# Attention and spatial gating on one core: a new plan of all calls, and the first batch's attention output copied out of PSUM before it is split

## The chip, the cores and the metric

The kernel runs on one core of one Trainium2 chip. The metric is device time of one execution in microseconds. The times shown are the median of three runs and their ends.

## The reference

The input is q, k, v of 4 batches x 8 heads x 768 positions x 64, all in float32. The attention is banded with a few global columns, and the output feeds a gated MLP with a spatial product over the positions:

```python
scores = q @ k.T / 8 - slope[h] * dist          # keep: column < n_global, or 0 <= row - col < n_local
a = softmax(where(keep, scores, -1e9))           # n_global = 8, n_local = 96
x = (a @ v), heads side by side                  # (4, 768, 512)
h = relu(x @ w_in)                               # w_in 512 x 1024; u, v = halves of h
v_n = (v - mean(v)) / sqrt(var(v) + 1e-6)        # over the 512 features
v_s = w_spatial @ v_n + b_spatial                # over the 768 positions
out = (u * v_s) @ w_out                          # w_out 512 x 512
```

w_in and w_out come as float64 and are read as pairs of 32-bit words.

## The kernel before

A batch is cut into six blocks of 128 positions, so there are 24 blocks n. With a band of 96 a block of queries needs its own block of keys and the one before, 256 columns in all; the global columns are copied into the previous block's first columns (kg into kring). Per block the steps are: P fetches q and k, W fetches v, S computes scores (PSUM tile s), evicts them on DVE with the bias and a running extreme (pr, mn), takes the exponential on ACT with a row sum, normalises (pr by rc), and A transposes the weights on TensorE (PSUM tile p), copies them to SBUF (pth), and multiplies with v (PSUM tile ops). Batch 0 does this with float32 operands. Batches 1 to 3 split k, q, v, and the transposed weights into a high and a low half in a reduced-precision format, by a cast and a subtraction (hi_lo), and gather q and k by DMAs through raw and rawh. Every x is split into xth and xtl.

The MLP runs over those halves with three products each (high x high, high x low, low x high): V gives v and its normalisation (row statistics st, mv, rs, then vnh, vnl), U gives u, G the spatial product over w_t (spatial weights) with the bias b_bc and the product with u, split into gh and gl, and O the output product with w_out. V is per block, U, G and O per 256 positions. Their PSUM tile is m, and ev is a ring of three staging tiles in SBUF. The weights are prepared during batch 0: I and Q split w_in and w_out (a bit-level conversion from float64, about ten 512- or 256-wide operations a piece, mostly on DVE), T splits w_spatial, B fetches the bias. The tiles u, raw, rawh and m serve the weights too, and blocks 4 and 5 of batch 0 keep their x in the tiles gh and gl.

No engine is programmed in the order of the source. A recorder keeps every call (that is why each row of the profile says line 39, where calls are issued), and a planner, run when the kernel is built, simulates five engines and a DMA queue with a cost for each call and puts the calls of each engine in the order in which its simulation starts them. Three tables steer it. KEYS gives each step a rank, and at equal readiness the lower one goes first. CFG says by letter which engine takes a kind of call: a (ACT), v (DVE), p (GpSimd, called POOL), or x, where the planner chooses; a string of several letters is taken in turn. The costs are in cost, reach and plan. Afterwards keep_warm looks at TensorE's planned gaps over a size, and fills them with transposes of the identity into a PSUM tile that nobody uses at that time (fillers: their only input is ident).

Of the kernel before, what the change touches and what calls it, by code (L numbers as in the profile page):

```python
# [263 lines left out]
def reach(op, o, eng, end, stand):  # L264

    if op.eng == "sync":
        return end if eng == "sync" and op.num not in o.after else stand + 50 + SLACK
    if op.eng == eng:
        return stand + 95 if op.num in o.after and eng != "tensor" else end
    return stand + CROSS[op.eng][eng] + SLACK  # L270


def plan(ops, keys, trace=None):
# [28 lines left out]
    while done < n:  # L302
# [79 lines left out]
def keep_warm(order, born, make):  # L382
# [7 lines left out]
    for op in order:  # L390
        if op.eng == "tensor":
            gap = op.begun - last
            if gap > WARM_GAP and op.begun < WARM_TO:
# [13 lines left out]
                if best and best[0] < last:  # L407
                    out.extend(make(best[1]) for _ in range(int((gap - 300) // 112)))
# [6 lines left out]
WORDS = {"gh": 1024, "gl": 1024, "pth": 1024, "vring": 3072, "kring": 2048, "pr": 256, "s": 512, "p": 512, "m": 512, "ops": 1024, "q0": 1024, "q1": 1024}  # L415
BUFS = {"gh": 1, "gl": 1, "u": 3, "s": 2, "p": 2, "m": 2, "raw0": 1, "raw1": 1, "rawh0": 1, "rawh1": 1}
SLACK = 120
KEYS = {('P', 0): 1.1, ('bias', 0): -1.7, ('S', 0): 0.03, ('bias', 1): 0.4, ('P', 1): 1.3, ('A', 0): -1.26, ('S', 1): 0.53, (0, 'T', 0): 1.88, (0, 'T', 1): 2.42, ('P', 2): 1.8, ('A', 1): 1.3, ('S', 2): 0.53, (0, 'V', 0): 1.99, (0, 'T', 2): 2.88, (0, 'T', 3): 2.38, ('P', 3): 2.3, ('A', 2): 2.3, ('S', 3): 3.03, ('W', 3): 3.2, (0, 'V', 1): 3.99, (0, 'U', 0): 2.14, (0, 'T', 4): 5.75, (0, 'T', 5): 3.88, ('P', 4): 4.99, ('A', 3): 3.3, ('S', 4): 3.53, ('W', 4): 2.77, (0, 'V', 2): 3.99, (0, 'Q', 0): 3.0, (0, 'Q', 1): 3.0, ('P', 5): 3.3, ('A', 4): 4.3, ('S', 5): 4.53, (0, 'V', 3): 4.99, (0, 'U', 1): 6.14, (0, 'Q', 2): 4.0, (0, 'Q', 3): 6.5, ('P', 6): 5.12, ('A', 5): 5.3, ('S', 6): 3.5, ('W', 6): 6.08, (0, 'V', 4): 5.99, (0, 'V', 5): 5.9, (0, 'U', 2): 8.14, ('P', 7): 5.62, ('A', 6): 6.04, ('S', 7): 6.0, ('W', 7): 7.08, (0, 'G', 0): 6.7, (0, 'O', 0): 6.5, ('P', 8): 7.12, ('A', 7): 6.96, ('S', 8): 5.5, ('W', 8): 8.58, (0, 'G', 1): 7.7, ('P', 9): 8.12, ('A', 8): 7.96, ('S', 9): 5.5, ('W', 9): 9.58, (0, 'G', 2): 8.7, (1, 'V', 0): 9.0, (1, 'V', 1): 9.34, (1, 'U', 0): 11.38, ('P', 10): 8.62, ('A', 9): 8.96, ('S', 10): 8.5, ('W', 10): 10.58, (1, 'V', 2): 10.0, ('P', 11): 10.12, ('A', 10): 9.96, ('S', 11): 9.5, ('W', 11): 11.08, (1, 'V', 3): 11.0, (1, 'U', 1): 12.0, ('P', 12): 10.13, ('A', 11): 10.96, ('W', 12): 13.08, (1, 'V', 4): 11.0, (1, 'V', 5): 13.0, (1, 'U', 2): 13.0, ('P', 13): 13.12, ('A', 12): 12.96, ('S', 13): 11.59, ('W', 13): 13.08, (1, 'O', 0): 14.16, ('P', 14): 13.12, ('A', 13): 12.96, ('S', 14): 12.5, ('W', 14): 13.08, (1, 'O', 1): 15.16, ('P', 15): 13.32, ('A', 14): 12.55, ('S', 15): 13.5, ('W', 15): 14.58, (1, 'G', 2): 15.0, (1, 'O', 2): 16.16, (2, 'U', 0): 16.5, ('P', 16): 15.12, ('A', 15): 14.96, ('S', 16): 15.71, ('W', 16): 15.55, ('P', 17): 15.62, ('A', 16): 15.96, ('S', 17): 15.5, ('W', 17): 15.58, (2, 'V', 3): 16.66, ('P', 18): 16.62, ('S', 18): 16.0, ('W', 18): 17.58, (2, 'V', 4): 17.0, (2, 'V', 5): 19.0, (2, 'U', 2): 19.5, ('P', 19): 18.12, ('A', 18): 17.96, ('S', 19): 17.5, ('W', 19): 17.29, (2, 'O', 0): 22.66, ('P', 20): 19.12, ('A', 19): 17.96, ('S', 20): 18.5, ('W', 20): 19.58, (2, 'G', 1): 19.5, (2, 'O', 1): 18.81, ('P', 21): 25.11, ('A', 20): 20.46, ('S', 21): 19.0, ('W', 21): 22.51, (2, 'G', 2): 21.0, (2, 'O', 2): 21.16, (3, 'V', 0): 18.71, (3, 'V', 1): 19.5, (3, 'U', 0): 23.74, ('P', 22): 20.62, ('A', 21): 20.96, ('S', 22): 20.5, ('W', 22): 22.08, (3, 'V', 2): 22.0, ('P', 23): 22.62, ('A', 22): 22.46, ('S', 23): 21.56, ('W', 23): 25.7, (3, 'V', 3): 22.5, (3, 'U', 1): 24.0, ('A', 23): 22.46, (3, 'V', 4): 23.0, (3, 'V', 5): 24.0, (3, 'O', 0): 25.16, (3, 'G', 1): 22.5, (3, 'O', 1): 25.85, (3, 'G', 2): 23.5, (3, 'O', 2): 27.12}
WARM_FROM, WARM_GAP, WARM_TO = 3000.0, 900.0, 150000.0
# [3 lines left out]
def attn_then_spatial_gating_kernel(  # L423
# [185 lines left out]
    def split_weights(src, hi, lo, st, x):  # L609
# [228 lines left out]
    def values(n):  # L838
# [23 lines left out]
        for g in range(NP):  # L862
# [7 lines left out]
            if whole(n):  # L870
# [322 lines left out]
```

## Time and profile before

| | |
|---|---|
| median of three runs | 508.26 us (506.62 to 509.0) |
| profiled execution | 506.37 us, span 504.6 us |
| TensorE (PE) busy | 481.6 us, 95% |
| VectorE (DVE) busy | 371.9 us, 74% |
| ScalarE (ACT) busy | 283.2 us, 56% |
| GpSimd (POOL) busy | 266.6 us, 53% |
| granted TensorE clock | 0.996 of full |

Times in the profile are in microseconds from the span's start; a mean time of one instruction is in nanoseconds. A row of a group gives line, engine, operation, output<-inputs, shapes and count, then busy time and mean, then the idle time of the engine just ahead and what ended it. In the windows the numbers behind a stretch are busy times of PE, the weight loads, DVE, ACT and POOL, with their instruction counts, then the granted clock, the DMA share and GB/s. Busy time of PE includes fillers.

### The profile page before, as it was taken

The numbers are of one execution on the slowest core, as the hardware profiler recorded it, in microseconds if no ns is written. First come the engines' busy times: TensorE is split into PE (matmuls) and PEld (weight loads), VectorE is DVE, ScalarE is ACT, GpSimd is POOL, SyncE is SP. The second block draws the span as 40 slices with busy tenths as digits, with TensorE's granted clock in tenths as the row PEclk, the third lists the DMA queues.
The fourth block names the chain that finished last, engine by engine and source line by source line (L and its number), as shares of the span: only waits on it lengthen the run. The fifth ranks groups of instructions, "written<-read, shape, count | busy, mean of one in ns | idle before, by whom it ended". The sixth has DMA issues, their size and how long they took to land.

```text
span 504.6 us, 10144 instructions
## 1 busy us (share of the span) xinstructions
PE 481.6 (95%) x3297; PEld 436.6 (87%) x3297; DVE 371.9 (74%) x1082; ACT 283.2 (56%) x779; POOL 266.6 (53%) x403
## 2 busy tenths in 40 slices
PE   8888999999998999999999999999989999999995
PEld 8776778879887988899989899998979989999994
DVE  5999979888478897787988765779877657743232
ACT  4568766653355777776667635777766516531111
POOL 3167544246446676789775634889765516241000
PEclk9899999999999999999999999999999999999999
DMA  6985510223776677666766626765657610000111
GB/s 203 286 202 144 142 33 20 70 60 107 177 191 160 161 200 202 163 174 163 179 162 178 184 73 170 199 170 148 168 128 206 163 58 1 12 2 1 43 43 48
DMA packets 68846, 65.51 MB, mean 130 GB/s; under 512 B 6736, under 2 KB 50000, under 8 KB 68784
## 3 DMA queue, kind: packets, MB, share of 16 engines
q1 hardware_dynamic: 68784, 64.78, 49.0%
q8 instruction: 28, 0.46, 0.4%
q14 instruction: 34, 0.28, 0.2%
HBM read 29.76 MB, written 6.68 MB: 72 GB/s over the span
## 4 chain that ended last, share of the span: by engine, by line
PE 68%; DVE 12%; DMA 6%; POOL 5%; ACT 4%; issue 2%; SPq 1%; POOLq 0%; ACTq 0%; DVEq 0%
PE m L39 49%; PE ops L39 8%; PE s L39 6%; PE p L39 5%; DVE ev L39 2%; DVE pr L39 2%; DMA raw<-in_k_dram 2%; POOL pr L39 2%; DMA kring<-raw 2%; ACT pr L39 2%; SPq L39 1%; DVE m L39 1%; DVE rawh L39 1%; DVE raw L39 1%; POOL raw L39 1%
## 5 line engine op out<-in xcount | busy, mean ns | idle before, releaser
L39 ACT ACTIVATE pr<-pr,mn 128x256 f32<-128x256 f32 (+1 forms) x192 | 92.0, 481 | 28.7 <-DVE mn L39 28.3
L39 POOL TENSOR_SCALAR pr<-pr,rc 128x256 f32<-128x256 f32 (+1 forms) x173 | 83.5, 503 | 8.1 <-DVE rc L39 6.5
L39 PE MATMUL s<-kring,q 128*128 128x256 f32 (+1 forms) x384 | 69.9, 307 | 6.1 <-DVE mn L39 4.3
L39 DVE CUSTOM_DVE_ANT_0 pr<-s,bias 128x256 f32<-128x256 f32 (+1 forms) x192 | 68.6, 395 | 7.6 <-PE s L39 6.3
L39 DVE TENSOR_TENSOR c<-ops,c 64x256 f32<-64x256 f32 x144 | 60.5, 420 | 14.2 <-ACT c L39 10.7
L39 PE MATMUL ops<-pth,vring 128*128 128x256 f32 x352 | 64.9, 313 | 4.8 <-ACT pth L39 1.4
L39 ACT ACTIVATE pth<-p 128x512 fp32r<-128x512 f32 (+3 forms) x96 | 52.4, 559 | 28.7 <-PE p L39 21.7
L39 PEld LDWEIGHTS s<-kring,q 128*128 128x128 f32 x384 | 56.0, 192 | 11.2 <-DVE mn L39 5.4
L39 PEld LDWEIGHTS ops<-pth,vring 128*128 128x128 f32 x352 | 50.6, 189 | 13.5 <-ACT pth L39 4.7
L39 PE MATMUL p<-ident,pr 128*128 128x128 f32 x352 | 58.2, 274 | 1.5 <-DVE pr L39 1.1
L39 DVE TENSOR_TENSOR pth<-p,pth 128x512 fp32r<-128x512 f32 (+1 forms) x72 | 45.8, 641 | 14.3 <-ACT pth L39 13.7
L39 PEld LDWEIGHTS p<-ident,pr 128*128 128x128 f32 x352 | 42.3, 140 | 8.0 <-DVE pr L39 1.6
L39 PE MATMUL m<-w_t_h,vnl 128*128 128x256 f32 x288 | 44.6, 282 | 0.0
L39 POOL TENSOR_TENSOR xtl<-c,xth 128x256 fp32r<-128x256 f32 x36 | 27.9, 775 | 31.5 <-ACT xth L39 31.3
L39 PE MATMUL m<-w_t_h,vnh 128*128 128x256 f32 x288 | 44.2, 284 | 0.0
L39 PE MATMUL m<-w_t_l,vnh 128*128 128x256 f32 x288 | 43.7, 282 | 0.0
L39 ACT ACTIVATE ev<-m 128x512 f32<-128x512 f32 (+1 forms) x37 | 21.5, 583 | 38.3 <-PE m L39 31.1
L39 POOL TENSOR_TENSOR vnl<-ev,vnh 128x512 fp32r<-128x512 f32 x24 | 31.5, 1313 | 19.0 <-ACT vnh L39 11.4
L39 PEld LDWEIGHTS m<-w_t_h,vnh 128*128 128x128 f32 x288 | 38.4, 189 | 0.7 <-ACT u L39 0.2
L39 DVE TENSOR_TENSOR ev<-m,b_bc 128x512 f32<-128x512 f32 x24 | 16.5, 689 | 30.4 <-PE m L39 30.3
L39 PEld LDWEIGHTS m<-w_t_h,vnl 128*128 128x128 f32 x288 | 38.5, 189 | 0.0
L39 PEld LDWEIGHTS m<-w_t_l,vnh 128*128 128x128 f32 x288 | 38.0, 189 | 0.0
(126 smaller groups left out, 1030.1 us busy)
## 6 DMA issues: line engine op xcount, KB each, us to landing
q<-rawh SPq DMA_DIRECT2D x72, 128.0 KB, 2.4
q<-raw SPq DMA_DIRECT2D x72, 128.0 KB, 2.4
out_dram<-ev SPq DMA_DIRECT2D x23, 256.0 KB, 2.7
raw<-in_q_dram SPq DMA_DIRECT2D x36, 128.0 KB, 3.0
raw<-in_v_dram SPq DMA_DIRECT2D x18, 256.0 KB, 3.3
raw<-in_k_dram SPq DMA_DIRECT2D x36, 128.0 KB, 3.0
kring<-rawh SPq DMA_DIRECT2D x36, 128.0 KB, 2.5
kring<-raw SPq DMA_DIRECT2D x36, 128.0 KB, 2.6
```

Of the source, the lines that this page charges most:

```text
L39: getattr(self.real, self.call)(*self.args, **self.kw)
```

## The change

All tables are replaced. CFG gets entries that hold for one batch only (a name with @ and the number), so that an engine choice can differ between batches; KEYS are new in nearly all entries. The planner's model of the DMA queue becomes a function, with an issue that can be held up by a full queue; keep_warm fills gaps from 500 ns of plan on instead of 900, and more densely. In the first batch the attention output is copied from PSUM to an SBUF tile (xs, of the ring c) and split there, in two whole 128 x 256 operations per pair of head pairs, where before each half of the partitions was split out of PSUM. The masking and the low word's scaling in the weight flush get a variant for GpSimd.

```diff
-CFG = {'vrelu': 'a', ... 'x0h': 'a', 'x0l': 'v', ... 'bias0': 'xx', 'bias1': 'vx', ... 'gm': 'x', ...}
+CFG = {'wf': 'v', 'wm': 'v', 'x0': 'a', ... 'bias0@0': 'a', 'bias1@0': 'p', 'bias2@0': 'a', ... 'x0@0': 'xxvv', 'xf0h@0': 'xx', 'xf0l@0': 'x', 'wf@0': 'vvvv', ... 'gm@1': 'v', 'gm@2': 'x', 'gm@3': 'p', ...}
...
+    more = SLACK_PE if eng == "tensor" else SLACK
...
+def transfer(op, t, queue):
+
+    end = t + min(max(op.busy, queue - 4500 - t), 1300)
+    queue = max(queue, t + 1200) + (op.late - 2050)
+    return end, queue + (1400 if t > 1500 else 3400), queue
...
         if e == "sync":
-            dma = max(dma, t + 1200) + (op.late - 2050)
-            stand = dma + 1400
+            end, stand, dma = transfer(op, t, dma)
...
-                    out.extend(make(best[1]) for _ in range(int((gap - 300) // 112)))
+                    out.extend(make(best[1]) for _ in range(int((gap - 200) // 112)))
...
-WARM_FROM, WARM_GAP, WARM_TO = 3000.0, 900.0, 150000.0
+WARM_FROM, WARM_GAP, WARM_TO = 3000.0, 500.0, 150000.0
...
     def E(key, k=0):
-        x = CFG[key]
+        x = CFG.get(f"{key}@{now_in[0]}", CFG[key])
         return EN[x[k % len(x)]]
...
-        nc.vector.scalar_tensor_tensor(out=a, in0=m, scalar=UPPER_MIN, in1=a, op0=ALU.is_ge, op1=ALU.mult)
+        if E("wf", x) is nc.gpsimd:
+            nc.gpsimd.tensor_scalar(out=m, in0=m, scalar1=UPPER_MIN, scalar2=1.0, op0=ALU.is_ge, op1=ALU.mult)
+            nc.gpsimd.tensor_tensor(out=a, in0=a, in1=m, op=ALU.mult)
+        else:
+            nc.vector.scalar_tensor_tensor(out=a, in0=m, scalar=UPPER_MIN, in1=a, op0=ALU.is_ge, op1=ALU.mult)
...
                 if g % 2:
-                    if folded(n):
-                        xs = work.tile([P, 2, P], F32, name="xs", tag="c1", bufs=nb("c1"))
+                    xs = work.tile([P, 2, P], F32, name="xs", tag="c1", bufs=nb("c1"))
                     for half, s_ in enumerate(halves):
...
-                            hi_lo(src, xh[s_, gs, toks], xl[s_, gs, toks], E("x0h", half), E("x0l", half))
-                    if folded(n):
-                        hi_lo(xs, xh[:, gs, toks], xl[:, gs, toks], E("xf0h", g // 2), E("xf0l", g // 2))
+                            cp(E("x0", half), xs[s_], src)
+                    hi_lo(xs, xh[:, gs, toks], xl[:, gs, toks], E("xf0h", g // 2), E("xf0l", g // 2))
...
```

TensorE counts the same useful instructions before and after; its fillers go from 181 to 229. What the new tables make of the order shows at three places. The first is the DMA queue of SyncE at the start of the program: before, the first instructions are these (nraw are the flags n_global and n_local, u a piece of w_in, vring a block of v).

```order
L39 DMA nraw<-in_n_global_dram 128x2
L39 DMA nraw<-in_n_local_dram 128x2
L39 DMA vring_112<-in_v_dram 128x512 x2
L39 DMA u_113<-in_moe_w_in_dram 128x1024
L39 DMA u_116<-in_moe_w_in_dram 128x1024
L39 DMA u_119<-in_moe_w_in_dram 128x1024
L39 DMA q_0_94<-in_q_dram 64x4x128
L39 DMA kring_96<-in_k_dram 64x4x128
L39 DMA q_0_94<-in_q_dram 64x4x128
L39 DMA kring_96<-in_k_dram 64x4x128
```

After, they stand so:

```order
L39 DMA vring_112<-in_v_dram 128x512
L39 DMA nraw<-in_n_global_dram 128x2
L39 DMA nraw<-in_n_local_dram 128x2
L39 DMA q_0_94<-in_q_dram 64x4x128
L39 DMA kring_96<-in_k_dram 64x4x128
L39 DMA q_0_94<-in_q_dram 64x4x128
L39 DMA kring_96<-in_k_dram 64x4x128
L39 DMA u_113<-in_moe_w_in_dram 128x1024
L39 DMA u_116<-in_moe_w_in_dram 128x1024
L39 DMA u_119<-in_moe_w_in_dram 128x1024
```

The first q and k transfers moved ahead of the three pieces of w_in, and one piece of v ahead of the flags.

The second place is ACT at the first attention output of batch 0 (ops is the output in PSUM, xth its high half, c the SBUF tile of the copies, w_in_h the high half of a weight piece). Before:

```order
L39 ACTIVATE pth_124<-p_123 128x256
L39 ACTIVATE pth_126<-p_125 128x256
L39 ACTIVATE pr_129,sums_92<-pr_129,mn_127 128x256
L39 ACTIVATE xth_121<-ops_93 64x2x128
L39 ACTIVATE pr_130,sums_92<-pr_130,mn_127 128x256
L39 ACTIVATE pth_124<-p_123 128x256
L39 ACTIVATE xth_121<-ops_93 64x2x128
L39 ACTIVATE pth_126<-p_125 128x256
L39 ACTIVATE w_in_h<-m_120 128x512
```

After:

```order
L39 ACTIVATE w_in_h<-m_114 128x512
L39 ACTIVATE w_in_h<-rawh_0_118 128x512
L39 ACTIVATE pth_124<-p_123 128x256
L39 ACTIVATE pth_126<-p_125 128x256
L39 ACTIVATE xth_121<-c_0_127 128x2x128
L39 ACTIVATE c_1_132<-ops_93 64x256 x2
L39 ACTIVATE xth_121<-c_1_132 128x2x128
L39 ACTIVATE w_t_h<-vring_112 128x768
L39 ACTIVATE pr_130,sums_92<-pr_130,mn_128 128x256
```

Casts out of ops have become copies of ops to c, and the cast reads c. On DVE, at the same place, before (xtl is the low half, rawh and m hold weight pieces):

```order
L39 TENSOR_TENSOR xtl_122<-ops_93,xth_121 64x2x128
L39 SCALAR_TENSOR_TENSOR m_120<-ev_99,m_120 128x512
L39 ISA pr_103,mn_127<-s_105,bias 128x256
L39 ISA mn_127 128x1
L39 TENSOR_SCALAR raw_0_115<-m_120 128x512
L39 TENSOR_TENSOR xtl_122<-ops_93,xth_121 64x2x128
L39 TENSOR_TENSOR m_120<-m_120,w_in_h 128x512
L39 TENSOR_TENSOR w_in_l<-rawh_0_118,ev_98 128x512
```

After:

```order
L39 COPY c_0_127<-ops_93 64x256 x2
L39 TENSOR_TENSOR m_114<-m_114,w_in_h 128x512
L39 TENSOR_SCALAR rawh_0_117<-rawh_0_118 128x512
L39 TENSOR_TENSOR xtl_122<-c_0_127,xth_121 128x2x128
L39 TENSOR_TENSOR w_in_l<-m_114,ev_97 128x512
L39 TENSOR_SCALAR raw_0_115<-m_120 128x512
L39 ISA pr_130,mn_128<-s_102,bias 128x256
L39 ISA mn_128 128x1
L39 TENSOR_TENSOR xtl_122<-c_1_132,xth_121 128x2x128
```

The subtraction that read ops now reads c, for all 128 partitions at once, and is done twice where it was done four times.

The third place is the end of the program on DVE, the last two gate products (u tiles hold u here) and the output copies. Before:

```order
L39 TENSOR_TENSOR ev_97<-m_114,b_bc 128x512
L39 TENSOR_TENSOR ev_97<-ev_97,u_116 128x512
L39 TENSOR_TENSOR gl_146<-ev_97,gh_145 128x512
L39 TENSOR_TENSOR ev_98<-m_120,b_bc 128x512
L39 TENSOR_TENSOR ev_98<-ev_98,u_116 128x512
L39 TENSOR_TENSOR gl_146<-ev_98,gh_145 128x512
L39 COPY ev_99<-m_114 128x512
```

After:

```order
L39 TENSOR_TENSOR ev_97<-m_114,b_bc 128x512
L39 TENSOR_TENSOR gl_149<-ev_97,gh_148 128x512
L39 TENSOR_TENSOR ev_98<-m_120,b_bc 128x512
L39 TENSOR_TENSOR gl_149<-ev_98,gh_148 128x512
L39 COPY ev_99<-m_114 128x512
```

and on POOL, whose last instructions before were those of the normalised v (vnl), there stand now:

```order
L39 TENSOR_TENSOR vnl_162<-ev_99,vnh_161 128x512
L39 TENSOR_TENSOR ev_98<-ev_98,u_119 128x512
L39 TENSOR_TENSOR ev_99<-ev_99,u_119 128x512
L39 TENSOR_TENSOR ev_99<-ev_99,u_113 128x512
L39 TENSOR_TENSOR ev_97<-ev_97,u_113 128x512
L39 TENSOR_TENSOR ev_97<-ev_97,u_116 128x512
L39 TENSOR_TENSOR ev_98<-ev_98,u_116 128x512
```

The products of the last batch with u have left DVE's order and close POOL's.

More of the change, by code (lines that the diff above doesn't have):

```diff
@@ L264, in reach @@
 def reach(op, o, eng, end, stand):
+    more = SLACK_PE if eng == "tensor" else SLACK
     if op.eng == "sync":
-        return end if eng == "sync" and op.num not in o.after else stand + 50 + SLACK
+        return end if eng == "sync" and op.num not in o.after else stand + 50 + more
     if op.eng == eng:
         return stand + 95 if op.num in o.after and eng != "tensor" else end
-    return stand + CROSS[op.eng][eng] + SLACK
+    return stand + CROSS[op.eng][eng] + more
+def transfer(op, t, queue):
+    end = t + min(max(op.busy, queue - 4500 - t), 1300)
+    queue = max(queue, t + 1200) + (op.late - 2050)
+    return end, queue + (1400 if t > 1500 else 3400), queue
 def plan(ops, keys, trace=None):
@@ L361, in plan @@
         begun[x] = t
-        free[e] = end = t + op.busy
-        stand = end + op.late
         if e == "sync":
-            dma = max(dma, t + 1200) + (op.late - 2050)
-            stand = dma + 1400
+            end, stand, dma = transfer(op, t, dma)
+        else:
+            end = t + op.busy
+            stand = end + op.late
+        free[e] = end
         done += 1
@@ L412, in keep_warm @@
     return out
[L415 removed]
+WORDS = {"gh": 1024, "gl": 1024, "pth": 1024, "vring": 3072, "kring": 2048, "pr": 256, "s": 512, "p": 512, "m": 512, "ops": 1024, "q0": 1024, "q1": 1024, "c1": 256}
 BUFS = {"gh": 1, "gl": 1, "u": 3, "s": 2, "p": 2, "m": 2, "raw0": 1, "raw1": 1, "rawh0": 1, "rawh1": 1}
 SLACK = 120
[L418 removed]
@@ L646, in split_weights @@
         nc.vector.scalar_tensor_tensor(out=ai, in0=ci, scalar=-0x40000000, in1=ai, op0=ALU.bitwise_and, op1=ALU.bitwise_or)
-        nc.vector.scalar_tensor_tensor(out=a, in0=m, scalar=UPPER_MIN, in1=a, op0=ALU.is_ge, op1=ALU.mult)
-        nc.vector.tensor_scalar(out=ci, in0=ai, scalar1=-0x800000, scalar2=None, op0=ALU.bitwise_and)
-        nc.vector.scalar_tensor_tensor(out=m, in0=lower.bitcast(U32), scalar=2.0 ** -52, in1=c, op0=ALU.mult, op1=ALU.mult)
+        if E("wf", x) is nc.gpsimd:
+            nc.gpsimd.tensor_scalar(out=m, in0=m, scalar1=UPPER_MIN, scalar2=1.0, op0=ALU.is_ge, op1=ALU.mult)
+            nc.gpsimd.tensor_tensor(out=a, in0=a, in1=m, op=ALU.mult)
+        else:
+            nc.vector.scalar_tensor_tensor(out=a, in0=m, scalar=UPPER_MIN, in1=a, op0=ALU.is_ge, op1=ALU.mult)
+        nc.vector.tensor_scalar(out=ci, in0=ai, scalar1=-0x800000, scalar2=None, op0=ALU.bitwise_and)
+        if E("wm", x) is nc.vector:
+            nc.vector.scalar_tensor_tensor(out=m, in0=lower.bitcast(U32), scalar=2.0 ** -52, in1=c, op0=ALU.mult, op1=ALU.mult)
+        else:
+            if E("wm", x) is nc.gpsimd:
+                nc.gpsimd.tensor_scalar(out=m, in0=lower.bitcast(U32), scalar1=2.0 ** -52, scalar2=1.0, op0=ALU.mult, op1=ALU.mult)
+            else:
+                nc.scalar.activation(m, lower.bitcast(U32), AF.Copy, scale=2.0 ** -52)
+            two(None, m, m, c, ALU.mult)
         cp(E("whi"), hi, a)
@@ L1032, in attn_then_spatial_gating_kernel @@
         more = n + 1 < B * NB
+        now_in[0] = b
         for tok in CFG["S" if b == 0 else "T"][i]:
```

5 lines of the change are left out of this document (4 added, 1 removed).

## The prediction

> **What bounds the kernel now.** I read the totals and the slices of the page first, then the busy times by stage, then who waits for whom, then the groups by form.
>
> ```profile
> PE 481.6 (95%) x3297; PEld 436.6 (87%) x3297; DVE 371.9 (74%) x1082; ACT 283.2 (56%) x779; POOL 266.6 (53%) x403
> PE   8888999999998999999999999999989999999995
> DVE  5999979888478897787988765779877657743232
> ```
>
> TensorE (PE) is busy 95% of 504.6 us and DVE 74%. A mean hides two regimes, so the stages:
>
> ```profile
> 0.00:10.00 10.00, 7.60 (x56) 7.60 (x57) 4.05 (x27) 2.47 (x7) 3.74 (x14) 1.00 0.52 189
> 10.00:60.00 50.00, 43.11 (x252) 35.47 (x251) 48.87 (x155) 35.09 (x107) 27.58 (x35) 0.97 0.82 209
> 60.00:120.00 60.00, 57.51 (x338) 48.45 (x338) 52.32 (x155) 36.50 (x94) 25.22 (x36) 1.00 0.17 50
> 140.00:400.00 260.00, 255.14 (x1832) 235.91 (x1833) 207.19 (x612) 171.76 (x485) 176.31 (x270) 1.00 0.66 168
> 400.00:440.00 40.00, 40.00 (x275) 36.94 (x274) 24.44 (x64) 19.57 (x48) 15.73 (x26) 1.00 0.14 43
> 440.00:490.00 50.00, 50.00 (x358) 47.07 (x357) 19.41 (x35) 8.89 (x17) 7.50 (x11) 1.00 0.06 22
> ```
>
> The columns behind the length are PE, weight loads, DVE, ACT, POOL. From 10 to 60 us DVE is busy 48.87 of 50: it evicts the scores, splits the weights and subtracts for the low halves, and PE waits for it. From 60 to 120 both are near full (57.51 and 52.32 of 60). From 140 on PE is the bound, and from 400 it has no hole. PE's busy time in the front is partly not work: fillers, which multiply the identity into a free bank.
>
> ```profile
> L39 PE MATMUL s<-ident 128*128 128x128 f32 x133 | 16.7, 288 | 2.4 <-POOL ident masks.py:199 2.4
> L39 PE MATMUL m<-ident 128*128 128x128 f32 x48 | 6.3, 288 | 0.0
> 2.40 13.14 PE L39 MATMUL s<-ident 128*128 128x128 f32 x105 [2.40 <-POOL ident masks.py:199]
> 6.01 0.17 DVE L39 CAST nf<-nraw 128x4 f32<-128x4 int32 x1 [5.06 <-DMA nraw<-in_n_local_dram]
> 119.59 0.76 PE L39 MATMUL m<-w_t_h,vnh 128*128 128x256 f32 x5
> 118.87 0.68 DVE L39 BATCH_NORM_STATS2 st<-ev 128x6 f32<-128x512 f32 x1
> ```
>
> The 181 fillers take 23.0 us, 0.127 us each, and PE starts on a real score at 15.4 us (2.40 and 13.14). So what there is to win lies mostly before 120 us. The last two rows give the mark at which I measure the front: the sixth row statistic of the first batch ends at 119.55 us, and the first spatial matmul follows at 119.59.
>
> **The change, part by part.** The new branches that let GpSimd flush the weights are not taken: the table says DVE for both switches, and the order shows both steps on DVE. They cost nothing. What acts is the copy in the first batch, the engine choices and the order. The sum is made against the profiled execution, 506.37 us (its span is 504.6), which is 1.9 us under the median of the runs, 508.26.
>
> *DVE work ahead of that mark.* I counted DVE's instructions up to the sixth statistic in both orders, and price what differs by these rows:
>
> ```profile
> L39 DVE TENSOR_TENSOR xtl<-ops,xth 64x256 fp32r<-64x256 f32 x16 | 6.7, 419 | 4.3 <-ACT xth L39 3.3 <-PE ops L39 0.9
> L39 DVE TENSOR_TENSOR gl<-ops,gh 64x256 fp32r<-64x256 f32 x8 | 3.4, 420 | 2.3 <-PE ops L39 2.2
> L39 DVE TENSOR_SCALAR bias<-ev 128x128 bf16<-128x128 f32 x4 | 0.8, 271 | 0.0
> L39 DVE TENSOR_SCALAR bias<-ev 128x256 bf16<-128x256 f32 x4 | 1.0, 284 | 0.0
> L39 DVE TENSOR_TENSOR w_out_l<-rawh,ev 128x256 fp32r<-128x256 f32 x4 | 2.8, 688 | 0.0
> L39 DVE TENSOR_TENSOR w_out_l<-m,ev 128x256 fp32r<-128x256 f32 x4 | 1.7, 414 | 0.0
> L39 DVE TENSOR_SCALAR u<-m 128x512 f32<-128x512 f32 x5 | 3.4, 685 | 0.3 <-PE m L39 0.2
> L39 DVE TENSOR_SCALAR pr<-pr,rc 128x128 f32<-128x128 f32 x4 | 1.9, 531 | 0.0
> L39 DVE TENSOR_SCALAR pr<-pr,rc 128x256 f32<-128x256 f32 x15 | 5.5, 395 | 0.0
> ```
>
> Gone are the 24 subtractions from PSUM (6.7 + 3.4 = 10.1 us) and all eight bias scalings (1.8 us), which go to ACT and POOL: -11.9. Added are eight of the new 128x256 subtractions (POOL takes the other four). No row has this one; between the two rows of w_out_l, 0.41 us with an operand in PSUM and 0.69 with both in SBUF, I take 0.69, since both of its operands lie in SBUF: +5.5 (3.3 at the low end). Two copies out of PSUM at 0.42: +0.8. Three more normalisations at 0.47 and three fewer at 0.37: +0.3. Two evictions with a maximum more and one fewer, at 0.69: +0.7. Some single casts and subtractions net +0.9 at 0.3 to 0.8 each. Together -3.7 us; -5.9 with the cheap subtraction, -2.0 if the new waits between ACT's copy and DVE's subtraction show. The mark moves with DVE's sum as long as DVE is nearly full up to it, which the windows say (105.24 of 120 us). The same count for the first eight weight pieces: the fifth is done with 6.3 us less DVE work ahead of it (seven score evictions and five subtractions now stand behind it), so the first MLP block can start that much sooner. **-3.7.**
>
> The Trainium skill (SBUF — State Buffer, Who interferes with whom) says that a DVE instruction with two SBUF inputs contends with a GpSimd instruction that reads SBUF, while one with at most one SBUF input, outside certain fast modes, does not. It speaks against moving the operand out of PSUM; the two rows of w_out_l agree with it (0.69 against 0.41), and without it this term would be -5.9.
>
> *The bank of the attention output.* Before, ops is free only after two ACT casts and two DVE subtractions; after, after two copies.
>
> ```profile
> PE ops L39 <- ACT xth L39: 1.0, 2, 0.7
> PE ops L39 <- ACT gh L39: 0.9, 2, 0.5
> PE ops L39 <- DVE xtl L39: 0.3, 1, 0.3
> L39 ACT ACTIVATE xth<-ops 64x256 fp32r<-64x256 f32 x16 | 6.0, 375 | 2.9 <-PE ops L39 1.7 <-DVE xtl L39 0.9
> ```
>
> PE lost 2.2 us to it (1.0 + 0.9 + 0.3); half of that I give to the stage before 60 us, where DVE would hold PE anyway. **-1.0** (0 to -2.2). On ACT 24 casts of 0.38 become 22 copies of that size and most of 12 whole casts, in a stage where it is busy 35.09 of 50 us: hidden; if that cover goes, ACT's copies are what ops waits for.
>
> *Start of the queue and fillers.* The first q and k transfers now go ahead of the three pieces of w_in; the two flags go behind one piece of v. The flags' landing starts the bias work (nf waits 5.06 us for it). One transfer more ahead of them: 0 to +1 us, covered in part because the scores no longer stand behind the first weight piece. I take 0. There are 48 more fillers; at 0.127 us that is +6.1 if they all stood on the path, and 0 if they only fill holes. PE's first run of them shrinks from 105 to 37 and the others grow, all ahead of the point where PE gets its first MLP block, and that point is set by DVE. **0** (0 to +6).
>
> *The middle, 140 to 400 us.* The whole order is new. PE idles 260 - 255.14 = 4.9 us there, and named waits are few:
>
> ```profile
> PE s L39 <- DMA kring<-raw: 1.6, 2, 1.4
> PE m L39 <- ACT gh L39: 1.3, 1, 1.3
> PE m L39 <- DVE gl L39: 0.8, 1, 0.8
> L39 DVE TENSOR_TENSOR raw<-raw,rawh 128x512 fp32r<-128x512 f32 x12 | 9.7, 806 | 1.7 <-ACT rawh L39 1.0 <-POOL rawh L39 0.6
> L39 POOL TENSOR_TENSOR raw<-raw,rawh 128x512 fp32r<-128x512 f32 x24 | 31.5, 1314 | 2.0 <-DVE rawh L39 0.7 <-ACT rawh L39 0.3
> L39 DVE TENSOR_TENSOR ev<-ev,u 128x512 f32<-128x512 f32 x24 | 19.2, 799 | 0.5
> ```
>
> Ten of the staging subtractions behind the kring transfer go from POOL (1.31) to DVE (0.81): 0.5 us sooner each time k or q is prepared. A new order can remove all of these holes or make as many: -4.9 to +5. I take half of the idle time as removed, since the wait for the kring transfer is what the shorter staging shortens and the other two came at places that no longer stand alike. **-2.5.** It is the weakest term.
>
> *The tail.* The gate product of the last batch is moved from DVE (0.69 here) to POOL, whose two-input operation of that size takes 1.31.
>
> ```profile
> 480.63 0.63 ACT L39 ACTIVATE gh<-ev 128x512 fp32r<-128x512 f32 x1 [3.69 <-DVE ev L39]
> 481.67 0.62 PE L39 MATMUL m<-w_out_h,gh 128*128 128x512 f32 x2
> 493.83 0.69 DVE L39 TENSOR_TENSOR ev<-ev,u 128x512 f32<-128x512 f32 x1
> 494.62 0.63 ACT L39 ACTIVATE gh<-ev 128x512 fp32r<-128x512 f32 x1 [3.69 <-DVE ev L39]
> 495.30 0.73 PE L39 MATMUL m<-w_out_h,gh 128*128 128x512 f32 x2
> ```
>
> At the last output block PE already starts 0.05 us behind gh (494.62 + 0.63, then 495.30), so the 0.62 us come in full. At the block before, gh ends at 481.26 and PE wants it at 481.67: 0.21 late, and the same at the first of the three. **+1.0** (+0.5 to +1.5). PE's order in the tail is unchanged.
>
> Sum: -3.7 - 1.0 + 0 - 2.5 + 1.0 = -6.2. From 506.37 that is 500.2; set beside the median, 508.26 - 6.2 = 502.
>
> **Rivals.** *More is won.* If the front follows the score chain and not DVE's sum, the 68 fillers fewer ahead of the first score are worth 68 x 0.127 = 8.6 us instead of 3.7 + 1.0, and the holes of the middle close altogether (-4.9): 508.3 - 8.6 - 4.9 + 1.0 = 496. For it: PE waits for its first score until 15.4 us. Against: DVE is 98% busy from 10 us on, and only its sum can shorten that.
>
> *Nothing is won.* From 60 to 120 us PE is busy 57.51 of 60. If that stage is already PE's, a sooner mark for DVE buys only the bank waits, and the fillers that outlast their holes give that back: -1.0 - 0.5 + 1.0 = 508.
>
> *Slower.* After the scores of the first batch DVE gets about 17 us more: 22 of the 128x256 subtractions (+15.2), ten staging subtractions (+8.1), less 13 gate products at 0.80 (-10.4), and smaller kinds that net about +4. Over 140 to 400 us it goes from 207.19 to some 222 of 260. It decides if the additions bunch, so that DVE stands in front of PE as it does at 10 to 60 us, and from 6.2 us of them on PE's path (with no gain in the middle) the change is slower; at six tenths it gives 508.3 - 3.7 - 1.0 + 1.0 + 10 = 515. For it: DVE is at 80% there already (207.19 of 260). Against: a sixth of its time would still be free.
>
> **How the numbers follow.** Half a per cent (2.5 us) is about what a measurement of this kernel can tell. Forecast (498 to 505.7 us): 0.48. More is won (under 498): 0.20. Nothing: 0.16, which I count as within half a per cent. Slower: 0.16. So faster 0.68, same 0.16, slower 0.16. The range: below, the first rival with the cheap subtraction and DVE's full gain (496 less the 2.2 between the two prices and some 4 for fillers that go too) is 490; above, fillers fully on the path (+6) with a middle 3 us worse than now is 502 + 2.5 + 3 + 6 = 513, and I stop at 512.
>
> **What the next profile would show.** Right: the first spatial matmul at about 115 instead of 119.6 us, the first score before 10 us, DVE still full from 10 to 60, no wait of ops for xth or gh before 110 us, PE idle under 4 us in the middle, gh about 0.6 us later against the last spatial matmul. Wrong: the mark not moved (then PE, not DVE, held the front), DVE at 95% in some stretch after 140 us, or new waits of PE for c or xtl, whose subtraction now stands behind a copy and a cast.

## The result and the profile after

The changed kernel takes 515.45 us (median of four runs, 513.96 to 517.22) against 508.04 us for the kernel before on the same chip (four runs; the 508.26 of the table is the median of the first three): a ratio of 1.015, interval 1.0107 to 1.0193, 7.4 us slower. The forecast was 502 us, and its range ended at 512. The profiled execution has a span of 512.9 us, 8.3 more than before.

From the page of the changed kernel, the totals and the slices of the span:

```profile
PE 487.2 (95%) x3345; PEld 444.2 (87%) x3345; DVE 384.6 (75%) x1097; ACT 273.0 (53%) x760; POOL 272.1 (53%) x407
PE   8999999999999898888999999999999999999995
DVE  3999988997688779898687898869884778852221
```

PE is as busy in share as before (95%), so the totals hide it. In the slices the front is fuller (the row begins with 8 and then only nines), and from 167 to 244 us stands a dent (898888) where the row of before has nines. Three of the stages of the prediction, in the changed kernel (busy time of PE, weight loads, DVE, ACT, POOL):

```profile
10.00:60.00 50.00, 47.33 (x326) 42.07 (x325) 45.88 (x141) 38.25 (x110) 28.86 (x35) 1.00 0.75 198
60.00:120.00 60.00, 60.00 (x378) 53.85 (x377) 55.80 (x157) 40.44 (x107) 32.13 (x44) 1.00 0.22 65
140.00:400.00 260.00, 245.49 (x1719) 223.65 (x1718) 210.32 (x611) 148.83 (x430) 157.68 (x245) 0.99 0.62 157
```

From 10 to 60 us DVE has 3.0 us less to do (45.88 after 48.87). In the middle PE idles 260 - 245.49 = 14.5 us where it idled 4.9. From 60 to 120 us PE has no hole left (60.00 of 60). The marks of the front in the changed kernel's timelines of PE and DVE:

```profile
2.41 7.08 PE L39 MATMUL s<-ident 128*128 128x128 f32 x37 [2.41 <-POOL ident masks.py:199]
9.33 1.06 PE L39 MATMUL s<-kring,q 128*128 128x128 f32 x8
111.61 0.69 DVE L39 BATCH_NORM_STATS2 st<-ev 128x6 f32<-128x512 f32 x1 [0.41 <-ACT ev L39]
114.84 0.64 PE L39 MATMUL m<-w_t_h,vnh 128*128 128x256 f32 x4
```

The first score comes at 9.33 us (15.4 before), the sixth row statistic ends at 112.3 (119.55 before, 7.2 sooner), and the first spatial matmul comes at 114.84 (119.59 before, 4.75 sooner). So the front gained at least what was forecast for it, and the loss lies behind it. The stretch with the dent, first before, then after (one row of the windows of each):

```profile
200.00:240.00 40.00, 39.39 (x284) 35.83 (x283) 31.53 (x94) 29.46 (x80) 34.37 (x55) 1.00 0.67 169
```

```profile
200.00:240.00 40.00, 33.39 (x221) 29.46 (x220) 34.95 (x96) 23.49 (x68) 31.29 (x48) 0.96 0.63 163
```

PE is busy 39.39 of 40 us before and 33.39 after: 6.0 us are gone here alone, and the granted clock is 0.96. What PE does at that place, in the changed kernel's timeline (start, duration, what the idle time ahead waited for):

```profile
204.22 0.72 PE L39 MATMUL s<-kring,q 128*128 128x256 f32 x4 [0.29 <-issue]
205.24 0.63 PE L39 MATMUL p<-ident,pr 128*128 128x128 f32 x4 [0.30 <-DVE pth L39]
206.29 1.43 PE L39 MATMUL s<-kring,q 128*128 128x256 f32 x8 [0.42 <-DVE mn L39]
209.24 0.78 PE L39 MATMUL p<-ident,pr 128*128 128x128 f32 x4 [1.52 <-DVE pth L39]
209.87 2.05 PE L39 MATMUL ops<-pth,vring 128*128 128x256 f32 x8
211.72 1.05 PE L39 MATMUL m<-w_in_h,xth 128*128 128x512 f32 x2
```

and in the timeline of before at the same time:

```profile
206.46 0.40 PE L39 MATMUL m<-w_in_l,xth 128*128 128x512 f32 x1
206.69 0.63 PE L39 MATMUL s<-kring,q 128*128 128x256 f32 x4
207.16 0.86 PE L39 MATMUL m<-w_in_l,xth 128*128 128x512 f32 x3
208.04 0.72 PE L39 MATMUL s<-kring,q 128*128 128x256 f32 x4
208.60 1.09 PE L39 MATMUL m<-w_in_h,xtl 128*128 128x512 f32 x4
209.54 0.63 PE L39 MATMUL m<-xth,w_in_l 128*128 128x256 f32 x4
210.00 0.63 PE L39 MATMUL s<-kring,q 128*128 128x256 f32 x4
```

Before, MLP matmuls (m) stand between the groups of scores, and while PE does them DVE evicts. After, PE's queue holds only attention from 204.2 to 211.7 us: scores, transposes, products with v, and the idle time ahead of three of the five groups ended with an answer of DVE. MLP work that could have stood between them had been done: the first V step of the second batch starts at 177.8 us instead of 188.8, while the last score eviction of each of the attention steps 9 to 12 comes only 0 to 2.8 us sooner. That the early MLP work makes the hole is a reading of these rows; the experiments come back to it. Who is waited for in the changed kernel from 195 to 240 us:

```profile
PE p L39 <- DVE pth L39: 1.8, 2, 1.5
PE ops L39 <- ACT ev L39: 1.7, 1, 1.7
PE p L39 <- DVE c L39: 1.3, 1, 1.3
PE ops L39 <- DVE c L39: 1.1, 1, 1.1
```

No single wait is large, and three of the four name DVE. Before, the named waits of PE in this stretch are two of 0.2 us.

### The profile page after: what moved, and what is told of

Its sections match the earlier page's. It is cut to its first block, busy times and chain, and to the rows that moved or that the text cites. A ratio compares the mean times of both kernels' runs of the same rounds, so it can differ in the third digit from the quotient of the medians.

```text
span 512.9 us, 10195 instructions
## 1 busy us (share of the span) xinstructions
PE 487.2 (95%) x3345; PEld 444.2 (87%) x3345; DVE 384.6 (75%) x1097; ACT 273.0 (53%) x760; POOL 272.1 (53%) x407
## 4 chain that ended last, share of the span: by engine, by line
PE 61%; DVE 11%; POOL 7%; SPq 5%; issue 5%; DMA 5%; ACT 5%; POOLq 0%; ACTq 0%
PE m L39 41%; PE ops L39 8%; PE s L39 7%; SPq L39 5%; PE p L39 5%; POOL pr L39 2%; DVE pr L39 2%; DMA raw<-in_k_dram 2%; DVE c L39 2%; DMA kring<-raw 2%; DVE raw L39 1%; DVE pth L39 1%; ACT pr L39 1%; DVE ev L39 1%; DVE m L39 1%
## 5 line engine op out<-in xcount | busy, mean ns | idle before, releaser
L39 POOL TENSOR_SCALAR pr<-pr,rc 128x256 f32<-128x256 f32 (+1 forms) x173 | 89.2, 536 | 40.7 <-DVE rc L39 29.5
L39 PE MATMUL ops<-pth,vring 128*128 128x256 f32 x352 | 63.4, 315 | 5.2 <-DVE c L39 2.0
L39 PEld LDWEIGHTS ops<-pth,vring 128*128 128x128 f32 x352 | 52.0, 193 | 10.8 <-ACT pth L39 2.6
L39 PE MATMUL p<-ident,pr 128*128 128x128 f32 x352 | 56.7, 275 | 4.4 <-DVE pth L39 1.8
L39 ACT ACTIVATE pth<-p 128x512 fp32r<-128x512 f32 (+3 forms) x83 | 45.0, 558 | 28.6 <-PE ops L39 19.3
L39 ACT ACTIVATE c<-ops 64x256 f32<-64x256 f32 x94 | 35.6, 379 | 23.1 <-PE ops L39 18.5
L39 PE MATMUL m<-w_t_h,vnl 128*128 128x256 f32 x288 | 43.5, 284 | 0.0
L39 ACT ACTIVATE gh<-ev 128x512 fp32r<-128x512 f32 x22 | 13.9, 632 | 54.4 <-POOL ev L39 38.2
L39 POOL TENSOR_SCALAR rawh<-raw 128x512 fp32r<-128x512 f32 x24 | 16.4, 685 | 43.7 <-DMA raw<-in_k_dram 18.8
```

What stands on the lines that cost most here:

```text
L39: getattr(self.real, self.call)(*self.args, **self.kw)
```

## The experiments

The expectations speak of lost time: the sum over PE's starts of what exceeds the spacing of dense matmuls of that shape. They number the theories: 1 is DVE as the engine that PE stands behind, 2 the written order of the later steps, 4 (further down) the front itself. A theory 3, that the staging chain and its transfers come late, was given no run of its own; of PE's named waits from 195 to 240 us in the changed kernel, 0.2 us are for a transfer. Ratios are to the kernel before, run on the same chip.

**Is it DVE, through engine choices?** That was the rival "slower" of the prediction, theory 1. The order is kept and single kinds of instruction change engine at their place, between the plan and its issue:

```diff
+    for op in order:                      # g_casts: steps ('A', 6) to ('A', 11)
+        if pth <- p on DVE:  op becomes the same copy on ACT          (13)
+    for op in order:                      # g_xtl: steps ('A', 12) and later
+        if xtl <- c, xth on DVE:  op becomes the same on GpSimd       (22)
+    for op in order:                      # g_gate: steps (3, 'G', j)
+        if ev <- ev, u on GpSimd:  op becomes the same on DVE         (6)
```

> The changed kernel with its order kept, instruction for instruction; the 13 casts of the transposed probabilities (pth<-p) that DVE has in the second batch go to ACT, each at its place. That takes 11 x 0.68 + 2 x 0.42 = 8.3 us off DVE between 150 and 235 us. Theory 1 (DVE is what PE stands behind at 200 to 235 us): PE's holes at 201 to 212 and 227 to 235 us, 12.2 us of lost time by PE's row of starts where the kernel before loses 4.4, shrink to about the latter, the V step of 225.5 us comes at 218 to 220, 506 to 509 us in all. Theory 2 (the order: PE's MLP work of the second batch is spent early, so that at 204 to 212 us only attention instructions, each waiting for the other, are left in PE's queue): the holes stay within 2 us, 513 to 517. Between them, 510 to 512: both.

> The changed kernel with its order kept; the 22 subtractions of the attention output (xtl) that DVE has in the third and fourth batch go to POOL, each at its place: 22 x 0.51 = 11 us off DVE, 22 x 0.8 = 18 us more on POOL. Theory 1 widened to 245 to 400 us, where another 5 us are lost: 508 to 512. Theory 2: 514 to 519, no gain, and a loss where POOL's longer operation comes later than DVE's.

> The changed kernel with its order kept; the six gate products of the last batch's own output blocks go from POOL (1.29) to DVE (0.72), each at its place. The prediction's term of the tail: 1.0 less (0.5 to 1.5), 514.4; PE's three waits for gh at the end (0.32, 0.28 and 0.93 us) gone but for about 0.3. If PE's clock or another step holds the tail: 515.4.

> The three edits of engines together (13 casts to ACT, 22 subtractions to POOL, 6 gate products to DVE), order kept. Theory 1: the gains add, 500 to 505 us, faster than the kernel before. Theory 2: the gate product's 1 us is all that comes, and POOL's longer subtractions may take it back: 513 to 518.

| | time, us | ratio |
|---|---|---|
| g_casts | 518.88 | 1.0192 (1.0156 to 1.0228) |
| g_xtl | 517.25 | 1.0155 (1.0114 to 1.0197) |
| g_gate | 515.6 | 1.0128 (1.0085 to 1.0171) |
| g_all | 517.85 | 1.0161 (1.0129 to 1.0192) |

Three earlier kernels, meant as the first three of these, issue the changed kernel's instructions without a difference, because the edit matched no step. They stand as repeats of it: 1.0128, 1.0167 and 1.0164, beside 1.0150. None of the four engine edits lies clearly outside that spread towards faster, and none reaches the times of theory 1. The times of g_xtl and g_all are those of theory 2; g_casts, at 518.88 us, lies above its 513 to 517. This row of the windows speaks against theory 1, from the run without the 13 casts on DVE:

```profile
200.00:240.00 40.00, 33.39 (x231) 29.74 (x232) 30.92 (x93) 26.87 (x75) 30.30 (x45) 1.00 0.63 157
```

DVE has 4.0 us less to do there (30.92 after 34.95), and PE is busy for 33.39 us, as it was. (The clock is 1.00 here, and ten more matmuls fit into the same time; a repeat of the changed kernel at a clock of 1.00 has 33.52 us and the same 231 matmuls.) Its waits in that stretch keep their names and nearly their size:

```profile
PE ops L39 <- DVE c L39: 2.1, 1, 2.1
PE ops L39 <- ACT ev L39: 1.9, 1, 1.9
PE p L39 <- DVE pth L39: 1.9, 2, 1.5
PE p L39 <- DVE c L39: 1.3, 1, 1.3
```

So this much less work on DVE does not shorten the stretch. The edit leaves a gap: in the narrow hole itself, from 205 to 210 us, DVE is still busy for 4.77 of 5 us without the casts (4.83 with them). A later run bears on it, k_best, whose order and engines are others throughout:

```profile
200.00:240.00 40.00, 37.57 (x278) 35.05 (x278) 38.65 (x123) 25.34 (x75) 19.23 (x29) 1.00 0.57 151
```

Its DVE is fuller here than the changed kernel's (38.65 us after 34.95), and PE is busy for 37.57. From 200 to 215 us its DVE is busy 14.55 of 15 us and PE 15.00; in the changed kernel they are 13.60 and 11.38. A full DVE alone does not make a hole. Whether less DVE work in just those 5 us would help the changed kernel's order was not run.

**The joined tables, planned anew.** The first batch by the new tables, all later steps by those of before, in the changed kernel's planner:

```diff
-CFG = {...}                      # the changed kernel's
-KEYS = {...}
+CFG = {later batches as before, entries @0 as in the changed kernel}
+KEYS = {steps of n < 6 and of the first batch's early MLP as in the changed kernel, the others as before}
```

> The changed kernel's code with its two tables joined: the first batch and the first six attention steps by the changed kernel's engine choices and order numbers, all later ones by those of the kernel before, planned anew. If the front of the change is worth what its mark shows (4.7 us) and what follows is as good as before: 502 to 504 us, faster than both. If the gain of the front is swallowed by whatever comes next (PE follows a chain that the front does not shorten): 507 to 509, as before. If the loss came from the front itself (work pulled forward there is missing later): 512 to 516.

512.41 us, 1.0055 (1.0031 to 1.0078): between both kernels. The time lies in the range that was set for a loss from the front itself (512 to 516), which the exchange below rules out. A hole stands again in the second batch, though not the same one. These two rows of the windows are of this kernel:

```profile
225.00:230.00 5.00, 1.63 (x4) 1.07 (x5) 3.26 (x8) 2.47 (x9) 5.00 (x6) 0.71 0.77 179
230.00:235.00 5.00, 5.00 (x21) 3.97 (x20) 0.38 (x1) 1.01 (x3) 3.43 (x9) 0.61 0.72 193
```

Here GpSimd is full (5.00) and PE waits. The old tables do not give the old order once something ahead of them has moved.

**Other tables.** Theory 2 is that the written order of the later steps costs; theory 4, that the front does, because whatever it wins comes back as waiting later. KEYS, or KEYS and engines, were searched by trying many sets in the planner. The third run searches the first batch too, so its front is not the same; its first spatial matmul comes at 115.1 us, close to the changed kernel's 114.84:

```diff
-KEYS = {...}
+KEYS = {steps behind the first batch: searched}               # k_keys
+KEYS, engines = {steps behind the first batch: searched}      # k_late
+KEYS, engines = {all steps: searched, from the joined tables} # k_best
```

> The changed kernel's code, its engine table and its order numbers up to the end of the first batch; the order numbers of all later steps are others, found by trying many sets of them in the planner of the kernel. Theory 2 (the written order of the later batches is what costs): PE's lost time at 200 to 240 us (12.2 us, where the kernel before loses 4.4) goes by half or more, 508 to 512 us, 4 to 7 less than the changed kernel. Theory 4 (the front is the cause: whatever it wins sends PE ahead of an attention whose pace is set elsewhere, by the staging transfers or DVE, and PE waits for the same later): 513 to 517, with as much lost between 160 and 300 us, only elsewhere.

> As the one before, but engine choices of the second to fourth batch are searched with the order numbers; first batch untouched. Theory 2: 504 to 509 us, PE's lost time behind 120 us (43.7 us in the changed kernel, 31.2 in the kernel before) back at 32 to 36, with the first spatial matmul still at about 115 us. Theory 4: 513 to 517.

> The changed kernel's code and its copy of the first batch's output; engine choices and order numbers of all steps searched anew, from the joined tables of the run that kept the first batch of the one and the rest of the other. Theory 2: the front's gain (about 4 us) stays and the later batches cost no more than before, 497 to 503 us, faster than both kernels. Theory 4: 507 to 512, since the later loss follows the front's gain.

519.87 us (1.0216, 1.0168 to 1.0264), 518.97 us (1.0193, 1.0143 to 1.0243) and 506.24 us (0.9961, 0.9935 to 0.9986). The first two miss the numbers of theory 2 and of theory 4: they are slower than the changed kernel, if anything. The third lies between theory 2's range (497 to 503) and theory 4's (507 to 512). It is a little faster than both kernels, so a front that is as early does not doom what follows. Together they say only that an order drawn anew can come out anywhere between 506 and 520 us.

**Exchanging the first batch, the order not planned anew.** This decides. Both plans are kept as lists of instruction, engine and time, cut behind the first batch (its last V and U step, attention steps 0 to 5), joined crosswise and issued in that order. Only the fillers are set anew, for the gaps of the joined list: 260 with the new front and the old rest, 175 the other way round, against 229 and 181:

```diff
-        for op in keep_warm(plan(nc.ops, KEYS), spare, filler):
+        for num, engine, at in KEPT:      # rows of the two plans, in order of time
+            op = nc.ops[num]
+            op.take(the way of that engine)
+            order.append(op)
+        for op in keep_warm(order, spare, filler):
```

> Two written orders joined at the end of the first batch, neither of them planned anew: the steps of the first batch up to its last V and U step stand as in the changed kernel (with its copy and engines), every later step stands with the engine and in the sequence that it has in the kernel before, 4 us of the timetable later. Theory 2 (the new order of the later steps costs some 12 us, the new front wins some 4): 502 to 506 us, 2 to 6 faster than before. Theory 4 (the front is the cause, whatever stands behind it): 512 to 516. The front's gain lost in the seam or by the pace of the attention: 507 to 510.

> The mirror: the first batch stands as in the kernel before, every later step with the engine and in the sequence of the changed kernel. Theory 2: 516 to 521 us, slower than both, since it has the new order's cost and not the front's gain. Theory 4: 507 to 510, as before.

> As the first of these three with the later steps 6 instead of 4 us later in the timetable, which is where no step has to be pulled ahead of another at the seam. Same expectations: theory 2 502 to 506, theory 4 512 to 516; a difference of more than 2 us from the first is the seam's.

| ratio to before | later steps as before | later steps as in the changed kernel |
|---|---|---|
| first batch as before | 1 | 1.0281 (1.0248 to 1.0314), 523.89 us |
| first batch as in the changed kernel | 0.9927 (0.9901 to 0.9952), 505.31 us | 1.0150 (1.0107 to 1.0193) |

With the later steps 6 instead of 4 us later at the cut: 0.9920 (0.9894 to 0.9947), 505.55 us, so the cut does not decide. Theory 2 holds in both rows in direction, and theory 4 in none; the old front with the new rest is slower still than theory 2's 516 to 521. The new front is worth 0.73% with the old rest (509.37 x 0.0073 = 3.7 us) and 1.3% with the new rest, and the new rest costs 2.2% behind the new front (11 us) and 2.8% behind the old one (14 us). The dent comes and goes with the rest. First the new front with the old rest, then the old front with the new rest:

```profile
200.00:240.00 40.00, 39.26 (x284) 36.50 (x284) 31.97 (x98) 28.62 (x80) 33.47 (x51) 1.00 0.66 163
```

```profile
200.00:240.00 40.00, 34.81 (x233) 30.85 (x232) 36.67 (x108) 25.35 (x79) 31.38 (x49) 0.96 0.70 173
```

The first of these is faster than both kernels, and the version to use (its interval overlaps that of k_best). In the profiles some of the front's gain does come back as waiting: its first spatial matmul is 4.5 us sooner than before (115.1), but from 140 to 400 us PE idles 7.5 us, where it idled 4.9, and the profiled spans, one execution each, differ by only 1.1 us (503.5 and 504.6; the one of before is 1.9 us faster than its median).

**Which part of the rest?** The same way of joining, now by batch, and with engines apart from sequence (123 later instructions have another engine in the two kernels):

```diff
+KEPT = first batch new, second batch new, third and fourth old      # s_second
+KEPT = first batch new, second batch old, third and fourth new      # s_last
+KEPT = first batch new, rest in old sequence, with new engines      # s_engines
+KEPT = all in new sequence, later steps with old engines            # s_sequence
```

> The joined order again (new front), with the steps of the second batch too as in the changed kernel (its V and U steps, attention steps 7 to 12, and the output blocks of the first), and only what follows as in the kernel before, 9 us of the timetable later. If the new order's cost lies in the second batch, as the changed kernel's lost time says (7.8 us more than before at 200 to 240 us, 6 more behind it): 511 to 515 us, 6 to 10 above the joined order. If it lies behind: 505 to 509.

> The other half: new front, second batch as in the kernel before, the third and fourth as in the changed kernel. If the cost lies in the second batch: 508 to 512 (the 6 us that the changed kernel loses behind 240 us, the gate products' 1.5 among them). If it lies behind: 512 to 517.

> The joined order (new front, old sequence behind it), but with the changed kernel's engine for each later instruction: 123 instructions change engine at their place. If sequence alone is the cause: 505 to 508. If the engine choices carry it: 513 to 518. If each table only fits the other: 515 and more, here and in the next.

> The reverse: the changed kernel's sequence for all steps, with the engine that the kernel before uses for each later instruction, the same 123. If sequence alone is the cause: 514 to 518, as the changed kernel. If the engine choices carry it: 504 to 508. If each table only fits the other: 520 and more.

| | time, us | ratio |
|---|---|---|
| s_second | 512.23 | 1.0067 (1.0036 to 1.0097) |
| s_last | 523.06 | 1.0282 (1.0226 to 1.0339) |
| s_engines | 517.04 | 1.0158 (1.0104 to 1.0211) |
| s_sequence | 526.85 | 1.0341 (1.0281 to 1.0402) |

The new second batch alone adds 1.4% to the joined order (7 us), and brings the dent. The row is of that run:

```profile
200.00:240.00 40.00, 33.97 (x222) 29.86 (x223) 31.90 (x91) 23.43 (x68) 30.02 (x44) 0.96 0.58 146
```

On PE the sequence of this run is the changed kernel's up to 214 us. From 200 to 215 us PE is busy 12.12 of 15 us, where the changed kernel has 11.38 and the joined order 14.73; the rest of the row stands behind the new cut.

The other half misses: with the new third and fourth batch the time is 523 us, more than either whole order behind this front, so the parts do not add. A cut inside the later steps joins steps that were never planned beside each other. That half's own row there is PE 35.82 of 40 us. Up to 207 us, where its sequence is still that of the joined order, PE is busy 7.00 of 7 us, and behind the cut 28.82 of 33, with DVE at 23.45 of 33: a hole with no full DVE. How much of 523 us is the third and fourth batch's and how much the cut's stays open.

Engines and sequence do not come apart either. The old sequence with the new engines loses 2.3% against the joined order; the new sequence with the old engines is 1.9% slower than the changed kernel, whose engines it gives back. Both times are in the ranges set for "each table only fits the other" (515 and more, 520 and more). So what is slow is the new pair of sequence and engines as a whole.

What in it leaves PE without work is not shown. The reading above, that MLP work is spent early, can't be the whole of it: in k_best the first V step of the second batch starts at 176.9 us, sooner still than the changed kernel's 177.8, and PE has no hole from 200 to 215 us. No run moves the MLP steps of the second batch and nothing else.

## Why the prediction was right and where it failed

*DVE work ahead of the sixth statistic, -3.7.* Right in mechanism, and too small. The statistic ends 7.2 us sooner, and DVE's busy time up to its end falls by 6.4 us (from 104.78 to 98.42), so the mark moved with DVE's sum. One reason for the size is the price of the new subtraction: 0.69 was taken, and the eight of them in the front took 4.0 us together, 0.50 each, nearer the low end. The group over the whole changed kernel says 0.51:

```profile
L39 DVE TENSOR_TENSOR xtl<-c,xth 128x256 fp32r<-128x256 f32 x27 | 13.7, 506 | 5.7 <-POOL xth L39 4.5 <-ACT xth L39 1.0
```

The rest of the gain did not reach the end. The first spatial matmul, taken in the prediction as following the statistic, comes 2.5 us behind it and only 4.75 us sooner than before, since PE has no hole from 60 us on. The exchange puts the whole front, forecast at -4.7 with the next term, at 3.7 us (2.4 to 5.0) with the old rest. That this is also the number of this term alone is chance.

*The bank of the attention output, -1.0.* The waits for xth, gh and xtl are gone, and one for c stands in their place, as the list of wrong signs had named. Up to 110 us in the changed kernel:

```profile
PE ops L39 <- DVE c L39: 0.9, 1, 0.9
PE ops L39 <- ACT pth L39: 0.7, 1, 0.7
```

For the bank that is 0.9 us where 2.2 stood, a gain of 1.3. The wait for pth is no new one: it was 1.4 us before. How much of this is separate from the term above was not measured.

*Start of the queue and fillers, 0.* There are 229 fillers instead of 181, and the front gained in spite of them. That they cost nothing was not measured by itself.

*The middle, -2.5: the step that failed.* All steps behind the first batch together measured +11 (+14 behind the old front). The tail's part of that is 1.6 us, so the middle is about +10; PE's idle time from 140 to 400 us says the same, 14.5 us where it was 4.9. The sentence "A new order can remove all of these holes or make as many: -4.9 to +5" took the old order's idle time as a measure for the new one in both directions. The idle time bounds the gain. It says nothing of the loss, which has no such bound: where PE's queue holds only steps that wait for one another, PE idles for as long as the answers take. The order of the changed kernel has such a stretch (scores, transposes and products with v alone, the rows at 204 to 212 us), and the term did not use it. That the new pair of sequence and engines costs this is shown; why just this pair does is open.

*The tail, +1.0.* The mechanism was right, and the size is 1.6: from the last product with v to the last output matmul it takes 56.66 us before and 58.24 in the changed kernel. The changed kernel's last output block, from its timeline:

```profile
501.91 1.29 POOL L39 TENSOR_TENSOR ev<-ev,u 128x512 f32<-128x512 f32 x1 [3.02 <-DVE ev L39]
503.23 0.63 ACT L39 ACTIVATE gh<-ev 128x512 fp32r<-128x512 f32 x1 [3.67 <-POOL ev L39]
503.91 0.74 PE L39 MATMUL m<-w_out_h,gh 128*128 128x512 f32 x2 [0.77 <-ACT gh L39]
```

and with the gate products back on DVE:

```profile
502.25 0.69 DVE L39 TENSOR_TENSOR ev<-ev,u 128x512 f32<-128x512 f32 x1
503.03 0.63 ACT L39 ACTIVATE gh<-ev 128x512 fp32r<-128x512 f32 x1 [3.69 <-DVE ev L39]
503.72 0.73 PE L39 MATMUL m<-w_out_h,gh 128*128 128x512 f32 x2
```

With them there, that stretch is 56.65 us again. The measured ratios, 1.0128 against 1.0150, cannot tell so little from nothing.

*The rival "slower" gave 515 us, and for a wrong reason.* It let DVE's work from 140 to 400 us grow from 207.19 to some 222; it is 210.32. It named "DVE at 95% in some stretch after 140 us", which came (9.65 of 10 us from 190 to 200), and "new waits of PE for c", which came too. Both signs came without the cause: with less work on DVE the stretch stays as it is, and with more of it (k_best) PE is busier. That its number agrees is chance.

## What to carry to other kernels

Where a change re-plans everything, the front that it is made for and the order that it happens to draw for the rest are two changes: price them apart, and let the second have a wide range on the side of loss, here up to 14 us in 508. Keep the old order of what the change does not touch as a written list and join it, since the old tables planned anew behind the new front gave 512 us and the kept list 505. And a wait names who came last, which need not be who is too slow: take work off that engine before believing it, and look for an order in which the same engine is as full and nobody waits.

## What was not expected of the hardware

*DVE beside GpSimd.* The subtraction raw<-raw,rawh of 128x512 on DVE, with both operands in SBUF, has a wide spread in the changed kernel. Three of its rows, each with what GpSimd did then:

```profile
193.13 0.75 POOL L39 TENSOR_TENSOR xtl<-c,xth 128x256 fp32r<-128x256 f32 x1
193.21 1.21 DVE L39 TENSOR_TENSOR raw<-raw,rawh 128x512 fp32r<-128x512 f32 x1
...
260.12 1.01 POOL L39 TENSOR_SCALAR pr<-pr,rc 128x256 f32<-128x256 f32 x1 [0.80 <-DVE rc L39]
260.19 0.68 DVE L39 TENSOR_TENSOR raw<-raw,rawh 128x512 fp32r<-128x512 f32 x1
...
295.80 1.31 POOL L39 TENSOR_TENSOR vring<-raw,vring 128x512 fp32r<-128x512 f32 x1
295.99 1.67 DVE L39 TENSOR_TENSOR raw<-raw,rawh 128x512 fp32r<-128x512 f32 x1
```

Beside a two-input operation of GpSimd it takes 1.06 to 1.67 us (eight rows, mean 1.30), beside the scaling pr<-pr,rc 0.68 to 0.84 (six rows, mean 0.74), beside another operation with one input 0.68 to 0.88 (three rows), and alone 0.68 to 0.69 (five rows). The Trainium skill (SBUF — State Buffer, Who interferes with whom) says that a DVE instruction with two SBUF inputs contends with a GpSimd instruction that reads SBUF. The trace agrees for GpSimd's two-input operations; beside its one-input operations the delay is absent in most rows and at most 0.2 us. The new subtraction is alike: eight of its 27 stood beside no GpSimd instruction at all and took 0.41 to 0.43, below the 0.69 of the forecast, and the longest (0.96 to 1.08) stood beside a two-input one for 0.68 to 0.79 us. Beside one-input operations alone it took 0.39 to 0.70 (nine rows).

*The clock behind a hole.* Two rows of the changed kernel's windows:

```profile
205.00:210.00 5.00, 2.82 (x17) 2.06 (x17) 4.83 (x21) 4.41 (x16) 4.92 (x7) 0.96 0.48 121
210.00:215.00 5.00, 5.00 (x23) 4.44 (x23) 4.61 (x13) 2.03 (x7) 3.32 (x6) 0.70 0.84 198
```

After five microseconds with PE busy for 2.82 the granted clock of the next five is 0.70, and eight products with v take 2.05 us there, where eight took 1.19 at 201.57 us. In one of the repeats of this kernel the hole is the same (3.05 of 5 us) and the clock stays at 1.00, at a span of 513.8 us against 512.9. So here the lower clock came with such a hole in one run and not in the other, and it does not explain the loss.
